# A fused attention and two-layer MLP kernel: every fourth addition into y goes from VectorE to a ScalarE copy and an accumulating DMA of GpSimd

## Chip, cores and metric

One core of a Trainium2 chip runs the whole kernel. The metric is the device time of one execution in microseconds (us). Engines are named as in the profile: PE (TensorE; PEld is its weight load), DVE (VectorE), ACT (ScalarE), POOL (GpSimd) and SP (SyncE, which here only issues DMAs).

## Reference

Attention over 4 sequences of 32 global and 512 local tokens, 8 heads of 64 (a local token sees the global tokens and the locals within 32 of it), and then two MLP layers with a squared ReLU:

```python
x = attn_out.transpose(0, 2, 1, 3).reshape(B * S, H * D)      # 2176 x 512
def _moe_ref(x, w_in, w_out):                                  # w_in 512 x 2048, w_out 2048 x 512
    h = x @ w_in
    r = np.maximum(h, 0.0)
    g = r * r
    return (g @ w_out).astype(np.float32)
x = _moe_ref(x=x, **moe_kwargs)
return _moe2_ref(x=x, **moe2_kwargs)                           # the same with other weights
```

## The kernel before

**Data.** Activations lie transposed: 512 features are four tiles of 128 partitions (index `d` or `k`), and the 2176 tokens are five blocks of 256, 512, 512, 448 and 448 columns (`NB`, blocks 0 to 4). Each fp32 operand is held as a high and a low part (`xh`/`xl`, `whi`/`wlo`, `gh`/`gl`), and each product is three matmuls (`three`, L565 to L567): high by high, high by low, low by high.

**Stages.** The first part is attention. The MLP then takes the 16 chunks of 128 hidden units of a layer two at a time. The first four chunks of layer 0 are done block by block; after them come 14 stages of two chunks each: 6 of layer 0 and 8 of layer 1. In a stage block 0 is computed directly (`first`), and the block pairs A = (1, 2) and B = (3, 4) by a scheme that trades products for sums of inputs and weights (`products`, `tsums`, `sums`). `activate` squares the ReLU and splits it (L585 to L591, L235). `second` multiplies the result by the chunk's `w_out` for each of the four `d`, into one PSUM bank for each: `Y0`, `PT0`, `PT1` and, for `d` = 3, `O0`.

**y.** `finish(d)` inside `second` moves a finished bank into the SBUF tile `y[b][:, d, :]`. For the first chunks of a layer it is a copy (L220). In the other stages, 6 of layer 0 and 7 of layer 1, it is an addition on DVE (L618): 13 stages x 5 blocks x 4 = 260 additions. After the last stage of layer 0 `y` is split into the inputs of layer 1 (L623, L625) and summed for the pairs (`tsums`, L725); after the last stage of layer 1 it is stored (L302).

**Staging tiles.** `staging()` hands out the `NR` tiles `r` of 128 x 512 in turn, to `activate` and to `products`.

**Order.** `Plan.add` records each operation with its engine, an assumed cost and a priority; `Plan.order` plays these costs forward, takes on each engine the ready operation of the best priority, and so fixes the order in which the instructions are written. Every engine then works through its own list strictly in that order. A changed cost or dependency therefore moves instructions on all engines from that point on.

```python
    def staging():
        i = cnt["r"] % NR
        cnt["r"] += 1
        return rt[i], ("r", i)
```

Of the kernel before, what the change touches and what calls it, by code (L numbers as in the profile page):

```python
# [13 lines left out]
AF = mybir.ActivationFunctionType  # L14
ALU = mybir.AluOpType
# [42 lines left out]
 'NS': 3,  # L58
 'NPT': 6,
 'NV': 2,  # L60
 'NR': 8,
 'NWR': 1,
 'NWT': 4,
 'Y': ['Y0'],
# [26 lines left out]
class Plan:  # L91
# [8 lines left out]
    def add(self, eng, cost, prio, fn, reads=(), writes=(), tail=0.0, lock=False, mode="M"):  # L100
        op = Op()
        op.eng, op.cost, op.prio, op.fn, op.tail, op.lock = eng, cost, prio, fn, tail, lock
        op.mode = mode
        op.seq = len(self.ops)
        deps = {}

        def dep(o, raw):
            if o is not None and o is not op:
                deps[o] = deps.get(o, False) or raw

        for r in reads:
            dep(self.writer.get(r), True)
        for w in writes:
            dep(self.writer.get(w), True)
            for o in self.readers.get(w, ()):
                dep(o, False)
        for r in reads:
            self.readers.setdefault(r, []).append(op)
        for w in writes:
            self.writer[w] = op  # L120
            self.readers[w] = []
        op.deps, op.users, op.left, op.ready = deps, [], len(deps), 0.0
        for o in deps:
            o.users.append(op)
        self.ops.append(op)
        return op

    def order(self):
        free, pend, avail = {}, {}, {}
        for op in self.ops:  # L130
            free.setdefault(op.eng, 0.55 if op.eng == "SP" else 0.0)
            pend.setdefault(op.eng, [])
            avail.setdefault(op.eng, [])
            if op.left == 0:
                heapq.heappush(pend[op.eng], (0.0, op.seq, op))
        done, dma, dmas, cols, port, tile_mode = [], 0.55, [], {}, {}, "M"
        while len(done) < len(self.ops):
            best = None
            for e in free:
                t = free[e] if avail[e] else (max(free[e], pend[e][0][0]) if pend[e] else None)  # L140
                if t is not None and (best is None or t < best[0]):
                    best = (t, e)
            t, e = best
            while pend[e] and pend[e][0][0] <= t:
                _, _, op = heapq.heappop(pend[e])
                heapq.heappush(avail[e], (op.prio, op.seq, op))
            op = heapq.heappop(avail[e])[2]
            if op.lock or e == "Pool":
                t = max(t, port.get("Pool" if e == "DVE" else "DVE", 0.0))
                port[e] = t + op.cost  # L150
            op.start, op.end = t, t + op.cost
            if e == "PE":
                n = int(t / TICK)
                op.end += switch(tile_mode, op.mode)
                tile_mode = op.mode
                if cols.get(n - 1, 0.0) < 3060:
                    op.end += op.cost * 0.95
                share, done_at = op.cost * 2400 / (op.end - t), t
                while done_at < op.end:
                    n = int(done_at / TICK + 1e-9)  # L160
                    upto = min(op.end, (n + 1) * TICK)
                    cols[n] = cols.get(n, 0.0) + share * (upto - done_at)
                    done_at = upto + 1e-9
            free[e] = op.end
            if e == "SP":
                if len(dmas) >= 8 and dmas[-8] > op.start:
                    op.start = dmas[-8]
                    free[e] = op.start + op.cost
                dma = max(dma, op.start + 1.1) + op.tail
                op.end = dma + 0.9  # L170
                dmas.append(op.end)
            done.append(op)
            for u in op.users:
                raw = u.deps[op]
                lat = LAT[e][u.eng] if u.eng != e or raw else 0.0
                u.ready = max(u.ready, op.end + lat)
                u.left -= 1
                if u.left == 0:
                    heapq.heappush(pend[u.eng], (u.ready, u.seq, u))
        self.total = max(o.end for o in done)  # L180
        return done


def switch(a, b):

    if a in "SVW":
        return 0.0 if a == b else 0.095 if b in "SVW" else 0.205 if b in "MG" else 0.145
    return 0.092 if b in "SVW" else 0.012 if a != b else 0.0


def dve(n, fast=False):
    return 0.065 + (0.53 if fast else 1.045) * n / 1000


def act(n):
    return 0.055 + 0.835 * n / 1000


def pe_r(n, m=128):
    return max(n + 32, 2 * m + 6) / 2400  # L200
# [3 lines left out]
def kernel(ctx: ExitStack, tc: tile.TileContext, kl, ql, vl, gk, gv, win, wout, msk, idn, out):  # L204
    nc = tc.nc
    plan = Plan()
    EARLY = CFG["EARLY"]
    add = plan.add
    picks = {}

    def pick(key):
        i = picks.get(key, 0)
        picks[key] = i + 1
        return CFG[key][i % len(CFG[key])]
# [40 lines left out]
    NR, NWR, NWT = (CFG[k] for k in ("NR", "NWR", "NWT"))  # L255
# [40 lines left out]
    def take(kind, names):  # L296
        k = names[cnt[kind] % len(names)]
        cnt[kind] += 1
        return k
# [264 lines left out]
    def three(out_, hi, lo, xhi, xlo, start, stop, again=False):  # L564
        nc.tensor.matmul(out=out_, lhsT=hi, rhs=xhi, start=start, stop=False, skip_group_check=again)  # L565
        nc.tensor.matmul(out=out_, lhsT=hi, rhs=xlo, start=False, stop=False, skip_group_check=again)  # L566
        nc.tensor.matmul(out=out_, lhsT=lo, rhs=xhi, start=False, stop=stop, skip_group_check=again)  # L567
# [5 lines that stand above are left out]
# [25 lines left out]
    def second(P, b, fs, slots, late, dfirst, stages):  # L598

        nb = NB[b]  # L600
        c3 = 3 * pe_r(nb)
        yk = [take("Y", CFG["Y"] + CFG["PT"] + CFG["O"] if late else CFG["Y"]) for _ in range(KD)]

        def passes(d, n):
            f, slot = fs[n], slots[n]
            o = bank[yk[d]][:, 0:nb]
            add("PE", c3, P(), lambda: three(o, wv(whi, slot)[:, d, :], wv(wlo, slot)[:, d, :], gh[f][:, 0:nb], gl[f][:, 0:nb],
                                             n == 0, n == len(fs) - 1), (("w", slot), ("gh", f), ("gl", f)), (yk[d],))

        def finish(d):  # L610
            o, yd = bank[yk[d]][:, 0:nb], y[b][:, d, :]
            Y = ("y", b, d)
            layer, begin, end = stages
            if begin:
                first = {1: (("gk", 0), ("gp", 0)), 2: (("gk", 1), ("gp", 1)), 3: (("gv", 0),), 4: (("gv", 1),)}.get(b, ())
                copy("yc", P(), yd, o, nb, (yk[d],), (Y,) + (first if layer == 0 else ()), psum=True)
                return
            add("DVE", dve(nb), P(), lambda: nc.vector.tensor_tensor(out=yd, in0=yd, in1=o, op=ALU.add), (yk[d],), (Y,))  # L618
            if end and layer == 0:
                if b in SECOND and d < 2:  # L620
                    return
                hi, lo = xh[b][:, d, :], xl[b][:, d, :]
                add("Activation", act(nb) + 0.04, P(), lambda: nc.scalar.activation(out=hi, in_=yd, func=AF.Copy),  # L623
                    (Y,), (("x", b, d),))
                add("DVE", dve(nb), P(), lambda: nc.vector.tensor_tensor(  # L625
                    out=lo, in0=yd, in1=hi.bitcast(F32), op=ALU.subtract), (Y,), (("x", b, d),), lock=True)
            elif end:
                load(P(), out[128 * d:128 * d + 128, OFF[b]:OFF[b] + nb], yd, 512 * nb, (Y,), ())

        N = len(fs)  # L630
        if dfirst:
            w = min(2, len(CFG["Y"]))
            for d0 in range(0, KD, w):
                for d in range(d0, d0 + w):
                    for n in range(N - 1):
                        passes(d, n)
                for d in range(d0, d0 + w):
                    passes(d, N - 1)
                    finish(d)
        else:  # L640
            for n in range(N):
                for d in range(KD):
                    passes(d, n)
                    if n == N - 1:
                        finish(d)
# [142 lines left out]
    for b in range(5):  # L788
        P = prios(MP[b], CFG["step"][b])
# [6 lines left out]
    for layer in range(2):  # L796
        for p in range(STAGES):
# [9 lines left out]
            for n, j in enumerate(order):  # L807
                P = prios(100 * (stage + 1) + 10 * n)
# [119 lines left out]
```

## Time and profile before

| | |
|---|---|
| median of 3 runs | 884.58 us (883.54 to 886.32) |
| profiled execution | 884.31 us, span 882.5 us from first to last instruction |
| granted TensorE clock | 1.00 |
| PE busy | 860.1 us, 97% of the span |
| DVE busy | 697.0 us, 79% |
| ACT busy | 551.3 us, 62% |
| POOL busy | 70.8 us, 8% |
| DMA | 67.92 MB, mean 77 GB/s |

Busy time says how long an engine had something in work, not whether it was waited for. "Idle before <- X" is time in which an engine stood still until X ended. The chain is followed back from the last instruction. The time outside the span (884.31 - 882.5 = 1.81 us) is start and end of the program.

### The profile page before, as it was taken

Reading aid. Unit: us, or ns where it says so; the run is one execution under the profiler, and the core shown is the slowest. Engines: PE = TensorE matmul, PEld = TensorE weight load, DVE = VectorE, ACT = ScalarE, POOL = GpSimd, SP = SyncE. Lnnn points to the kernel's source line nnn. Section 1 sums busy time; section 2 is a strip of 40 time slices with the busy share of each in tenths; the row PEclk is TensorE's granted clock in tenths of the full one; section 3 lists DMA queues with packets and bytes.
Section 4 is the critical chain, followed back from the end, with each engine's and each line's share of the span. In section 5 each row is a group of like instructions: output and inputs, shape, how many; then the busy total and the mean of one; then the engine's idle time right before and its main releaser. Section 6 shows DMA issues by size and latency. Waiting matters only on the chain.

```text
span 882.5 us, 14400 instructions
## 1 busy us (share of the span) xinstructions
PE 860.1 (97%) x5248; PEld 743.1 (84%) x5248; DVE 697.0 (79%) x1619; ACT 551.3 (62%) x1234; POOL 70.8 (8%) x116
## 2 busy tenths in 40 slices
PE   5999899999999999999999999999999999999998
PEld 4878686788888888898889889898988988898987
DVE  4988888753899798886877999788887777877544
ACT  4898789885675556535645779755554645554543
POOL 3333334320000000000000000000000000000000
PEclk9999999999999999999999999999999999999999
DMA  7877354420001121211110102112112020201023
GB/s 276 289 231 234 111 145 134 139 59 22 1 1 48 48 72 50 70 49 48 46 51 25 48 1 66 54 53 69 48 48 72 25 72 25 72 25 49 1 84 120
DMA packets 28071, 67.92 MB, mean 77 GB/s; under 512 B 3168, under 2 KB 13024, under 8 KB 28000
## 3 DMA queue, kind: packets, MB, share of 16 engines
q1 hardware_dynamic: 28000, 67.01, 24.2%
q8 instruction: 41, 0.67, 0.3%
q14 instruction: 30, 0.25, 0.1%
HBM read 62.54 MB, written 4.46 MB: 76 GB/s over the span
## 4 chain that ended last, share of the span: by engine, by line
PE 84%; ACT 6%; DVE 5%; DMA 3%; issue 1%; SPq 0%; POOL 0%; ACTq 0%; DVEq 0%
PE h L565 7%; PE h L566 7%; PE h L567 7%; PE PT L566 6%; PE PT L565 6%; PE PT L567 6%; PE S L565 5%; PE S L566 5%; PE S L567 5%; PE Y L565 4%; PE Y L566 4%; PE Y L567 4%; PE O L566 3%; PE O L567 3%; PE O L565 3%; PE O L382 2%
## 5 line engine op out<-in xcount | busy, mean ns | idle before, releaser
L235 DVE TENSOR_TENSOR gl<-r,gh 128x448 fp32r<-128x448 f32 (+2 forms) x160 | 96.6, 610 | 59.2 <-ACT r L589 57.9
L566 PE MATMUL PT<-gl,whi 128*128 128x448 f32 (+2 forms) x288 | 103.5, 359 | 0.0
L565 PE MATMUL PT<-gh,whi 128*128 128x448 f32 (+2 forms) x288 | 103.4, 359 | 0.0
L567 PE MATMUL PT<-gh,wlo 128*128 128x448 f32 (+2 forms) x288 | 103.3, 359 | 0.0
L520 ACT ACTIVATE whi<-wt 128x512 fp32r<-128x512 f32 x92 | 56.9, 623 | 73.6 <-PE S L566 34.6
L586 ACT ACTIVATE gh<-r 128x448 fp32r<-128x448 f32 (+2 forms) x160 | 89.1, 562 | 2.4 <-PE Y L567 0.2
L585 ACT ACTIVATE r<-r 128x512 f32<-128x512 f32 (+1 forms) x84 | 50.5, 601 | 61.7 <-DVE r L695 61.3
L589 ACT ACTIVATE r<-r 128x448 f32<-128x448 f32 (+2 forms) x145 | 82.2, 568 | 3.8
L565 PE MATMUL h<-xh,whi 128*128 128x512 f32 (+2 forms) x232 | 83.6, 360 | 0.6 <-ACT r L585 0.6
L618 DVE TENSOR_TENSOR y<-y,PT 128x448 f32<-128x448 f32 (+2 forms) x130 | 75.5, 600 | 9.2 <-PE PT L567 8.9
L566 PE MATMUL h<-xl,whi 128*128 128x512 f32 (+2 forms) x232 | 80.3, 346 | 2.4 <-DVE xl L396 2.3
L567 PE MATMUL h<-xh,wlo 128*128 128x512 f32 (+2 forms) x232 | 79.9, 344 | 0.0
L565 PE MATMUL Y<-gh,whi 128*128 128x512 f32 (+2 forms) x208 | 76.8, 369 | 0.2 <-ACT y L220 0.2
L566 PE MATMUL Y<-gl,whi 128*128 128x512 f32 (+2 forms) x208 | 75.0, 361 | 0.5 <-DVE gl L235 0.5
L235 DVE TENSOR_TENSOR wlo<-wt,whi 128x512 fp32r<-128x512 f32 x92 | 63.2, 690 | 14.8 <-ACT whi L520 14.4
L567 PE MATMUL Y<-gh,wlo 128*128 128x512 f32 (+2 forms) x208 | 74.6, 359 | 0.0
L351 ACT ACTIVATE s<-s,mn 128x224 f32<-128x224 f32 x128 | 60.2, 473 | 8.9 <-DVE mn L346 8.8
L565 PE MATMUL S<-xh,whi 128*128 128x448 f32 (+2 forms) x184 | 65.5, 356 | 0.0
L566 PE MATMUL S<-xl,whi 128*128 128x448 f32 (+2 forms) x184 | 65.3, 355 | 0.0
L567 PE MATMUL S<-xh,wlo 128*128 128x448 f32 (+2 forms) x184 | 65.1, 354 | 0.0
L566 PEld LDWEIGHTS PT<-gl,whi 128*128 128x128 f32 x288 | 54.3, 188 | 6.5 <-DVE gl L235 0.2
L565 PEld LDWEIGHTS PT<-gh,whi 128*128 128x128 f32 x288 | 54.3, 188 | 6.4
(129 smaller groups left out, 2125.0 us busy)
## 6 DMA issues: line engine op xcount, KB each, us to landing
wraw<-win SPq DMA_DIRECT2D x32, 512.0 KB, 3.5
wraw<-wout SPq DMA_DIRECT2D x32, 512.0 KB, 3.5
v<-vl SPq DMA_DIRECT2D x32, 224.0 KB, 2.7
rk<-kl SPq DMA_DIRECT2D x32, 192.0 KB, 2.9
y<-gk SPq DMA_DIRECT2D x8, 672.0 KB, 5.5
y<-gv SPq DMA_DIRECT2D x8, 640.0 KB, 6.9
rq<-ql SPq DMA_DIRECT2D x32, 128.0 KB, 2.5
out<-y SPq DMA_DIRECT2D x8, 256.0 KB, 2.0
```

The costliest lines, as they stand in the source:

```text
L235: add("DVE", dve(n), prio, lambda: nc.vector.tensor_tensor(out=get(out_), in0=get(a), in1=get(b), op=ALU.subtract), reads, writes, lock=True)
L351: add("Activation", 0.48, P(), lambda t=t, sb=sb: nc.scalar.activation(out=st[sb][:, t, :], in_=st[sb][:, t, :], func=AF.Exp, bias=mn[sb][ ...
L382: nc.tensor.matmul(out=bank[ok][64 * e:64 * e + 64, 128 * t:128 * t + 128], lhsT=vt[vb][:, 128 * k + 64 * e:128 * k + 64 * e + 64], rhs=pt ...
L520: nc.scalar.activation(out=whi[slot], in_=tf, func=AF.Copy)
L565: nc.tensor.matmul(out=out_, lhsT=hi, rhs=xhi, start=start, stop=False, skip_group_check=again)
L566: nc.tensor.matmul(out=out_, lhsT=hi, rhs=xlo, start=False, stop=False, skip_group_check=again)
L567: nc.tensor.matmul(out=out_, lhsT=lo, rhs=xhi, start=False, stop=stop, skip_group_check=again)
L585: add("Activation", act(nb), P(), lambda: nc.scalar.activation(out=r, in_=src, func=AF.Relu), (S,), (R,))
L586: add("Activation", act(nb) + 0.04, P(), lambda: nc.scalar.activation(out=a, in_=r, func=AF.Square), (R,), (("gh", f),))
L589: add("Activation", act(nb) + 0.04, P(), lambda: nc.scalar.activation(out=r, in_=r, func=AF.Square), (), (R,))
L618: add("DVE", dve(nb), P(), lambda: nc.vector.tensor_tensor(out=yd, in0=yd, in1=o, op=ALU.add), (yk[d],), (Y,))
```

## The change

A new setting `ya` = 'DDDM' is stepped through by the additions of `finish`. Since each block has four of them, the fourth, `d` = 3, always gets M: ACT copies bank `O0` to a staging tile, and POOL issues a DMA that adds this tile to `y[b][:, 3, :]` in SBUF. That is 65 of the 260 additions: 13 of 256, 26 of 448 and 26 of 512 columns. The staging tiles go from 8 to 7, the build's parameter `dynamic_dma_scratch_size` from 256 to 2048. The planner books the DMA with 1.2 on POOL and 3.0 more until it has landed; these two numbers are assumptions written in the code.

```diff
- 'NR': 8,
+ 'ya': 'DDDM',
+ 'NR': 7,
...
+            if e == "Pool":
+                op.end += op.tail
...
-            add("DVE", dve(nb), P(), lambda: nc.vector.tensor_tensor(out=yd, in0=yd, in1=o, op=ALU.add), (yk[d],), (Y,))
+            if pick("ya") == "M":
+                r, R = staging()
+                r = r[:, 0:nb]
+                add("Activation", act(nb), P(), lambda: nc.scalar.activation(out=r, in_=o, func=AF.Copy), (yk[d],), (R,))
+                add("Pool", 1.2, P(), lambda: nc.gpsimd.dma_start(out=yd, in_=r, accum_op=ALU.add), (R,), (Y,), tail=3.0)
+            else:
+                add("DVE", dve(nb), P(), lambda: nc.vector.tensor_tensor(out=yd, in0=yd, in1=o, op=ALU.add), (yk[d],), (Y,))
...
-    nc = _bacc.Bacc("TRN2", target_bir_lowering=False, num_devices=1, dynamic_dma_scratch_size=256)
+    nc = _bacc.Bacc("TRN2", target_bir_lowering=False, num_devices=1, dynamic_dma_scratch_size=2048)
```

In the changed kernel lines stand 3 to 9 further down: L220 is L223 there, L585 is L588, L618 is L627, and the new copy and DMA are L624 and L625. PE runs the same matmuls; their order is the same through attention and the first chunks and differs in places after that. The rows below are the instructions as written, with the semaphores that each waits for in brackets (Activation_49 is ACT's counter, DMASW a DMA issued by POOL, DMAHW one issued by SP).

**The end of the program.** The last rows of DVE before; `O_156` is the bank of `d` = 3, `y_74` is block 0:

```order
L235 TENSOR_TENSOR gl_86<-r_90,gh_82 128x256 [waits Activation_49]
L618 TENSOR_TENSOR y_74<-y_74,Y_151 128x256 [waits PE_49]
L618 TENSOR_TENSOR y_74<-y_74,PT_154 128x256 [waits PE_49]
L618 TENSOR_TENSOR y_74<-y_74,PT_155 128x256 [waits PE_49]
L618 TENSOR_TENSOR y_74<-y_74,O_156 128x256 [waits PE_49]
```

The last rows of ACT now (`O_155` is the same bank):

```order
L624 ACTIVATE r_91<-O_155 128x512 [waits DVE_49,PE_49]
L588 ACTIVATE r_89<-S_151 128x256 [waits DMASW4_49,PE_49]
L589 ACTIVATE gh_81<-r_89 128x256 [waits Activation_49]
L588 ACTIVATE r_90<-S_152 128x256 [waits PE_49]
L589 ACTIVATE gh_82<-r_90 128x256 [waits Activation_49]
L592 ACTIVATE r_90<-r_90 128x256 [waits Activation_49]
L624 ACTIVATE r_92<-O_155 128x256 [waits PE_49]
```

The last rows of POOL now:

```order
L625 DMA y_77<-r_89 128x448 [waits DMASW2_49,Activation_49]
L625 DMA y_78<-r_87 128x448 [waits DMASW3_49,Activation_49]
L625 DMA y_75<-r_88 128x512 [waits DMASW0_49,Activation_49]
L625 DMA y_76<-r_91 128x512 [waits DMASW7_49,DMASW1_49,Activation_49]
L625 DMA y_74<-r_92 128x256 [waits Activation_49]
```

The last addition of the program has moved from DVE to a copy on ACT and a DMA on POOL.

**The stores behind it.** SP's last rows before:

```order
L302 DMA out<-y_76 128x512 [waits DMAHW1_49,DVE_49]
L302 DMA out<-y_74 128x256 [waits DMAHW2_49,DVE_49]
L302 DMA out<-y_74 128x256 [waits DMAHW3_49,DVE_49]
L302 DMA out<-y_74 128x256 [waits DMAHW4_49,DVE_49]
L302 DMA out<-y_74 128x256 [waits DMAHW5_49,DVE_49]
```

And now:

```order
L305 DMA out<-y_76 128x512 [waits DMAHW1_49,DMASW7_49]
L305 DMA out<-y_74 128x256 [waits DMAHW2_49,DVE_49]
L305 DMA out<-y_74 128x256 [waits DMAHW3_49,DVE_49]
L305 DMA out<-y_74 128x256 [waits DMAHW4_49,DVE_49]
L305 DMA out<-y_74 128x256 [waits DMAHW5_49,DMASW0_49]
```

The very last store now waits for a DMA of POOL to have landed, where it waited for DVE.

**A staging tile taken again.** ACT in the first of the 14 stages, now (`r_91` receives a bank of `d` = 3 and is written again five rows later):

```order
L624 ACTIVATE r_91<-O_155 128x512 [waits PE_49]
L523 ACTIVATE whi_101<-wt_96 128x512 [waits DVE_49]
L624 ACTIVATE r_89<-O_155 128x512 [waits PE_49]
L223 ACTIVATE r_87<-h_149 128x448 [waits PE_49,Activation_49]
L588 ACTIVATE r_92<-r_92 128x448 [waits DVE_49]
L223 ACTIVATE r_91<-h_148 128x512 [waits DMASW1_49,PE_49,Activation_49]
```

ACT at the same place before:

```order
L494 ACTIVATE wraw_95<-wraw_95 128x512 [waits DMAHW7_49,DVE_49]
L520 ACTIVATE whi_107<-wt_97 128x512 [waits DVE_49]
L585 ACTIVATE r_93<-r_93 128x448 [waits DVE_49]
L220 ACTIVATE r_94<-h_150 128x448 [waits PE_49]
L586 ACTIVATE gh_81<-r_93 128x448 [waits Activation_49]
L589 ACTIVATE r_93<-r_93 128x448 [waits Activation_49]
L220 ACTIVATE r_89<-h_149 128x512 [waits PE_49]
```

The copy of a PSUM bank of products into `r_91` (L223) now waits for the DMA that reads the tile's earlier content; before, such copies waited for PE and the compute engines alone. In all, 4 of the 65 tiles are written again on ACT within 10 rows, and 9 within 15.

## Rows read from the trace of the kernel before

**Rows 1.** The page: span, and busy time of each engine.
```profile
span 882.5 us, 14400 instructions
PE 860.1 (97%) x5248; PEld 743.1 (84%) x5248; DVE 697.0 (79%) x1619; ACT 551.3 (62%) x1234; POOL 70.8 (8%) x116
```

**Rows 2.** Busy time by stretch (start:end, length, engines, PEclk, DMA share, GB/s).
```profile
250.00:300.00 50.00, 48.61 (x240) 42.03 (x239) 47.18 (x88) 31.34 (x60) 0.00 (x0) 1.00 0.11 32
500.00:550.00 50.00, 50.00 (x254) 44.10 (x253) 49.85 (x89) 40.52 (x81) 0.00 (x0) 1.00 0.11 32
850.00:882.50 32.50, 28.70 (x149) 24.51 (x147) 14.41 (x25) 10.86 (x20) 0.00 (x0) 1.00 0.32 118
300.00:850.00 550.00, 549.80 (x2805) 486.31 (x2804) 445.97 (x812) 310.64 (x590) 0.00 (x0) 1.00 0.16 48
```

**Rows 3.** Waits of PE from 230 us on (total us, times, longest).
```profile
PE S L565 <- ACT r L220: 1.4, 2, 0.7
PE Y L566 <- DVE gl L235: 0.5, 2, 0.3
PE Y L565 <- ACT y L220: 0.2, 1, 0.2
```

**Rows 4.** Groups by form: DVE's additions from bank O (busy us, mean ns | idle before).
```profile
L618 DVE TENSOR_TENSOR y<-y,O 128x512 f32<-128x512 f32 x26 | 17.7, 680 | 4.0 <-PE O L567 4.0
L618 DVE TENSOR_TENSOR y<-y,O 128x448 f32<-128x448 f32 x26 | 15.9, 613 | 1.8 <-PE O L567 1.8
L618 DVE TENSOR_TENSOR y<-y,O 128x256 f32<-128x256 f32 x13 | 5.4, 414 | 0.6 <-PE O L567 0.6
```

**Rows 5.** Groups by form: ACT's copies out of bank O.
```profile
L220 ACT ACTIVATE y<-O 128x512 f32<-128x512 f32 x2 | 1.2, 604 | 0.8 <-PE O L567 0.8
L220 ACT ACTIVATE y<-O 128x448 f32<-128x448 f32 x3 | 1.6, 538 | 0.1
L220 ACT ACTIVATE y<-O 128x256 f32<-128x256 f32 x1 | 0.4, 384 | 0.3 <-PE O L567 0.3
```

**Rows 6.** Timeline of PE, bank O used twice near the end (start us, us).
```profile
867.59 0.39 PE L567 MATMUL O<-gh,wlo 128*128 128x512 f32 x1
867.82 0.39 PE L565 MATMUL Y<-gh,whi 128*128 128x512 f32 x1
...
871.90 0.39 PE L565 MATMUL O<-gh,whi 128*128 128x512 f32 x1
```

**Rows 7.** Timeline of the last 5 us: last matmul, last addition, last stores.
```profile
878.40 1.79 SPq L302 DMA_DIRECT2D out<-y  x4
...
878.71 0.28 PE L567 MATMUL O<-gh,wlo 128*128 128x256 f32 x1
879.02 0.42 DVE L618 TENSOR_TENSOR y<-y,O 128x256 f32<-128x256 f32 x1
```

**Rows 8.** One line's instructions, SP's stores: duration min/median/max ns; landing us.
```profile
L302 SPq DMA_DIRECT2D out<-y x20: 332/333/403, 847.4 to 879.8; - x20
DMA to landing us min/median/max: 1.7/2.0/2.2
```

**Rows 9.** DMA issues (KB each, median us from issue to landing).
```profile
y<-gk SPq DMA_DIRECT2D x8, 672.0 KB, 5.5
...
out<-y SPq DMA_DIRECT2D x8, 256.0 KB, 2.0
...
out<-y SPq DMA_DIRECT2D x4, 128.0 KB, 1.8
```

**Rows 10.** Groups by form on POOL, the longest of it.
```profile
L238 POOL TENSOR_TENSOR lk<-rk,hk 128x384 fp32r<-128x384 f32 x21 | 23.4, 1113 | 14.8 <-DVE hk L223 7.7 <-issue 2.8 <-ACT hk L220 2.0
```

**Rows 11.** Groups by form on DVE from 200 us on: first step of the weights.
```profile
L484 DVE TENSOR_SCALAR wt<-wraw 128x512 uint32<-128x512 uint32 x52 | 21.9, 422 | 10.5 <-DMA wraw<-wout 6.0 <-DMA wraw<-win 4.0
```

## The prediction

> **What bounds the kernel now.** I read the page's busy times first [rows 1]: PE has work for 860.1 of 882.5 us, DVE for 697.0, ACT for 551.3, and POOL for 70.8. A share over the whole span says little, so the second view is busy time by stretch [rows 2]. From 300 to 850 us, which holds nearly all additions into y, PE is busy 549.80 of 550 us at a granted clock of 1.00, with DVE at 445.97 and ACT at 310.64. The reader is to see that DVE may be full for 50 us (49.85 from 500 to 550) while PE still misses nothing. The third view, the waits of PE [rows 3], gives what a faster DVE or ACT could return after 230 us: 1.4 + 0.5 + 0.2 = 2.1 us, of which 1.4 stand behind ACT. That a busy PE could hide waits is a fair objection; matmuls on 512 columns start 0.23 us apart (867.59 and 867.82 [rows 6]), and 512 columns at 2.4 GHz are 0.213 us, so little is hidden. The kernel is bound by PE up to its last matmul; behind that stands a tail that nothing covers [rows 7]. It is the place to price.
>
> **The base.** The profiled execution took 884.31 us: span 882.5 and 1.81 around it. The median of the runs is 884.58, so 0.27 above; I add to 884.31. What can be told from no change is 0.3%, here 2.65 us.
>
> **DVE loses 65 additions.** By form [rows 4]: 26 x 0.680 + 26 x 0.613 + 13 x 0.414 = 17.7 + 15.9 + 5.4 = 39.0 us less on DVE. Worth on the path: 0. PE runs beside them; the most they could give back is the 0.5 us in which PE waited for DVE [rows 3].
>
> **ACT gains 65 copies.** The same copy exists in the kernel, from bank O with the same three widths [rows 5]: 26 x 0.604 + 26 x 0.538 + 13 x 0.384 = 15.7 + 14.0 + 5.0 = 34.7 us more on ACT. Cost on the path: 0, hidden by PE, since ACT has 239 us free from 300 to 850 [rows 2]. If that cover goes, the copy is late and PE waits for bank O. Near the end the last matmul on O starts at 867.59 and ends at 867.98, and the next one on O starts at 871.90 [rows 6]: 3.9 us, for a copy of 0.6, so some five queued ACT operations fit ahead of it.
>
> **POOL gains 65 DMAs**, and nothing stands in their way there: its 70.8 us belong to attention, and from 250 us on it does nothing [rows 1, 2]. They carry 14.5 MB (26 x 256 KB + 26 x 224 KB + 13 x 128 KB), and the DMA must read y as well, while the engines' queues are 16% busy between 300 and 850 us [rows 2]. Cost 0; weights could come a little later, and nobody is near that bound.
>
> **Staging tiles.** Seven instead of eight, 65 more takers, and a tile is free only when the DMA has read it. The list of ACT in the changed program shows 4 of the 65 tiles written again within 10 rows, the closest five rows later. At some 0.6 us a row that is 3 us, in an engine that works strictly in order; behind a late tile its squares and weight copies queue up, and PE waits for those. With the DMA length I take below this costs at most a few tenths: 0 in the sum. The splits of y between the layers also wait for such DMAs, but the inputs are needed by PE later than the DVE work that lies between; also 0.
>
> **The end.** Here every step lies on the path. Before [rows 7]: the last matmul starts at 878.71 and ends at 878.99, DVE adds from 879.02 to 879.44, and SP's four stores end their issue at 878.40 + 1.79 = 880.19. With 0.33 for an issue [rows 8] the last one starts at 879.86, 0.42 after the addition; it ends the span 2.3 us later, at 882.5. Now ACT copies in 0.384 instead of DVE's 0.414 [rows 4, 5]: nothing gained or lost. POOL then has to notice, issue, and the DMA has to land before SP may start the last store. For noticing I take what SP needed behind DVE, 0.42. For issue to landing no row shows a DMA of POOL or one that adds. The lower end is SP's own store of the same 128 KB: 1.8 [rows 9]. The upper end is its load of 672 KB, five times the bytes: 5.5 [rows 9]. I take 3.1, nearer the lower end because the bytes are those of the short row: 1.8, plus 1.1 for POOL to prepare it (its slowest group of instructions takes 1.113 each [rows 10]; what an issue costs it no row shows), plus 0.2 because y is read too (256 KB against 128 KB on SP: 2.0 against 1.8 [rows 9]). The tail grows by 0.42 + 3.1 = **3.5 us**, with ends at 2.2 and 5.9. The planner's own assumption of 1.2 + 3.0 would make it 4.6.
>
> The Trainium skill (DMA: Bandwidth & Descriptors, section on the anatomy of a DMA on the GpSimd path) has a fit of 2.0 us plus bytes / 436e3 for such a DMA: an estimate of 2.3 us for 131,072 bytes. By it the sum below would be 887.0, inside what counts as no change. No run here shows a DMA of POOL yet.
>
> **Sum.** 884.31 + 0 (DVE) + 0 (ACT) + 0 (POOL, staging) + 3.5 (end) = **887.8 us**, 3.2 above the median (0.36%). With the ends of the DMA's length: 886.5 to 890.2.
>
> **Rivals.**
>
> *The end is short, and a relieved DVE helps (not slower).* One mechanism: the DMA takes about what SP's stores take, so the tail grows by 2.2 to 2.7 us. In addition the stretch from 250 to 300 us may run better, where DVE is 94% busy and PE idle for 1.39 us [rows 2]. For it: the same bytes leave SBUF in 1.8 us on SP, and that stretch does depend on DVE. Against: the 1.4 us there stand behind ACT [rows 3], which gets no relief, one staging tile fewer makes such waits likelier, and POOL's preparation is left out. It gives 885.1 (1.4 won, 2.2 lost) to 887.0. It decides at a growth of the tail of 2.9 us: below that, the time is within 0.3% of 884.58. Chance 0.36, in which I count the short end of my own range. The fit of the Trainium skill above falls in this case.
>
> *Faster.* To get below 881.9 the program must win 2.4 us and the tail's growth back, at least 4.6 together. PE's waits after 230 us are 2.1 [rows 3], and earlier the program is the same. That leaves only waits hidden in busy time. Chance 0.04.
>
> *The DMAs land late, and the staging tiles bind (slower by more).* If a DMA takes 6 us or more in the middle of the program, the tiles taken again within 10 rows come late by some 3, 2, 1 and 1 us, ACT stands still, and PE waits for about half of it: 3 to 4 us, on top of a longer tail of up to 6. It gives 890 to 894. What could do it: weight loads of 512 KB in front of it on the same engines, or DVE. For it: POOL's part is unknown here. Against: the planner places each reuse where its assumed 4.2 us have passed, so the wait begins only beyond that. It decides at about 5 us from issue to landing. Chance 0.12.
>
> The Trainium skill (SBUF — State Buffer, section on the two separate sides) says that GpSimd cannot write the descriptors of a DMA while DVE runs an operation in a mode that takes both ports, and would have them late in this way. The trace so far has no such DMA; DVE's operations of the likely kind take 0.42 us each [rows 11], so one of them alone delays little.
>
> *The forecast itself*, a tail of 2.9 to 5.9 and little else: 0.48, all of it slower by over 0.3%.
>
> **How the numbers follow.** Slower by over 0.3%: 0.48 + 0.12 = 0.60. Within 0.3%: 0.36. Faster: 0.04. The predicted time is that of the likeliest case, 887.8. The range reaches down into the short tail, to 885.4, and up through the longer DMA into half of the late one, to 892.0; about one in ten is left out on either side. The likeliest case alone lies at 887.2 to 890.2.
>
> **What would show it.** In the changed profile: DVE down by about 39 us and ACT up by about 35; 65 DMAs on POOL with a landing time of about 3 us for 128 KB; PE still over 549 of 550 us from 300 to 850; and in the last 8 us the order matmul, ACT copy, DMA of POOL, last store, with 7.0 us from the end of the last matmul to the end of the span, against 3.5 before (878.99 to 882.5). The forecast is wrong if PE shows waits for ACT that end with DMASW events between 250 and 850 us, if the tail grows by under 2.9 us, or if PE's part before the last matmul gets shorter by more than 2 us.

## The result, and the profile after

| | before | changed |
|---|---|---|
| median, 18 runs each on the same chips | 885.98 us (882.56 to 889.05) | 892.24 us (887.84 to 896.80) |
| ratio, 95% interval | | 1.0070 (1.0053 to 1.0088) |
| profiled execution | 884.31 us, span 882.5 | 887.84 us, span 886.0 |

The change costs 6.3 us by the medians. The forecast was 887.8 with a range of 885.4 to 892.0: the sign was right, the size half of what came, and the time lies just outside the range. Of the 4.4 us between 892.24 and 887.8, 1.7 lie in the base: the sum started at the profiled execution, 884.31, and the kernel before has a median of 885.98 here. The first profiled execution took 887.84, the forecast to the hair, and that is an accident: it is the fastest of its 18 runs. Its attention part was 2.4 us faster than in the profile of before, with the same instructions in the same order: the two traces first differ at about 223 us, on DVE. Against the prediction stands the median.

The page of the changed kernel answers to [rows 1]:

```profile
span 886.0 us, 14604 instructions
## 1 busy us (share of the span) xinstructions
PE 860.5 (97%) x5248; PEld 742.8 (84%) x5248; DVE 667.3 (75%) x1554; ACT 584.8 (66%) x1299; POOL 128.6 (15%) x181
```

The 65 additions left DVE (1554 instructions for 1619), the 65 copies came to ACT, PE has the same work. Busy time by stretch in the changed kernel, as [rows 2] (DVE, ACT and POOL are the third to fifth busy times, then PEclk, DMA share, GB/s):

```profile
300.00:850.00 550.00, 547.97 (x2795) 484.65 (x2794) 420.68 (x757) 341.01 (x649) 48.24 (x56) 1.00 0.30 70
850.00:886.00 36.00, 29.59 (x154) 25.32 (x152) 12.78 (x22) 13.00 (x24) 4.07 (x5) 0.98 0.51 148
```

Between 300 and 850 us PE now misses 2.03 us, where it missed 0.20 [rows 2]; the DMA engines are busy 30% where it was 16%. The waits of PE from 230 us on, as [rows 3]:

```profile
PE h L568 <- ACT r L223: 1.4, 2, 0.9
PE h L568 <- ACT r L588: 0.9, 1, 0.9
PE S L568 <- ACT r L223: 0.7, 1, 0.7
PE Y L569 <- DVE gl L238: 0.6, 2, 0.3
PE PT L569 <- DVE gl L238: 0.2, 1, 0.2
PE S L568 <- DVE r L704: 0.2, 1, 0.2
```

That is 4.0 us in place of 2.1. The end of the program in the timeline (start us, us), as [rows 7]:

```profile
878.75 4.90 SPq L305 DMA_DIRECT2D out<-y  x5
...
879.60 0.28 PE L570 MATMUL O<-gh,wlo 128*128 128x256 f32 x1
879.92 0.38 ACT L624 ACTIVATE r<-O 128x256 f32<-128x256 f32 x1 [2.13 <-PE O L570]
880.66 0.86 POOL L625 DMA_DIRECT2D y<-r  x1 [4.35 <-ACT r L624]
```

From the start of the last matmul to the end of the span it is 886.0 - 879.60 = 6.40 us, where it was 882.5 - 878.71 = 3.79 [rows 7]: 2.6 us more. The new DMAs themselves, in the page's list of DMA issues (KB, median us to landing) and as the instructions of their line (duration min/median/max in ns, then landing in us):

```profile
y<-r POOLq DMA_DIRECT2D x26, 256.0 KB, 3.3
...
y<-r POOLq DMA_DIRECT2D x26, 224.0 KB, 3.2
...
y<-r POOLq DMA_DIRECT2D x13, 128.0 KB, 2.7
```
```profile
L625 POOL DMA_DIRECT2D y<-r x65: 852/862/1087, 271.4 to 880.7; - x65
...
DMA to landing us min/median/max: 2.6/3.3/6.0
```

To compare executions I cut each in three: **attention**, to the start of its last group of matmuls (L382 before, L385 in the changed kernel); **body**, from there to the start of the last matmul of the program; **tail**, from there to the end of the span. Each cut is a start time on PE in the timeline. For attention these are, before and in the changed kernel:

```profile
217.59 1.09 PE L382 MATMUL O<-pt,v 112*64 112x128 f32 x16
```
```profile
215.19 1.09 PE L385 MATMUL O<-pt,v 112*64 112x128 f32 x16
```

| kernel | tiles | adds by DMA | attention | body | tail |
|---|---|---|---|---|---|
| before | 8 | 0 | 217.59 | 661.12 | 3.79 |
| changed | 7 | 65 | 215.19 | 664.41 | 6.40 |

So 2.6 us were lost in the tail and 3.3 in the body; attention hid 2.4 of them.

### The profile page after: what moved, and what is told of

It reads as the page before. It is cut to its first block, busy times and chain, and to the rows that moved or that the text cites. A ratio compares the mean times of both kernels' runs of the same rounds, so it can differ in the third digit from the quotient of the medians.

```text
span 886.0 us, 14604 instructions
## 1 busy us (share of the span) xinstructions
PE 860.5 (97%) x5248; PEld 742.8 (84%) x5248; DVE 667.3 (75%) x1554; ACT 584.8 (66%) x1299; POOL 128.6 (15%) x181
## 4 chain that ended last, share of the span: by engine, by line
PE 79%; DVE 8%; ACT 6%; DMA 4%; issue 2%; SPq 0%; POOL 0%; POOLq 0%; ACTq 0%; DVEq 0%
PE h L568 7%; PE h L569 7%; PE h L570 7%; PE PT L568 6%; PE PT L570 6%; PE PT L569 6%; PE S L568 4%; PE S L569 4%; PE S L570 4%; PE Y L568 4%; PE Y L569 4%; PE Y L570 4%; PE O L568 3%; PE O L570 3%; PE O L569 3%; PE O L385 2%
## 5 line engine op out<-in xcount | busy, mean ns | idle before, releaser
L625 POOL DMA_DIRECT2D y<-r x65 | 56.8, 874 | 616.2 <-ACT r L624 569.8
L624 ACT ACTIVATE r<-O 128x512 f32<-128x512 f32 (+2 forms) x65 | 34.6, 533 | 118.9 <-PE O L570 118.9
L627 DVE TENSOR_TENSOR y<-y,PT 128x448 f32<-128x448 f32 (+2 forms) x130 | 76.2, 605 | 19.2 <-PE PT L570 18.6
L588 ACT ACTIVATE r<-r 128x512 f32<-128x512 f32 (+1 forms) x84 | 50.4, 600 | 28.7 <-DVE r L704 28.6
```

The costliest lines, as they stand in the source:

```text
L588: add("Activation", act(nb), P(), lambda: nc.scalar.activation(out=r, in_=src, func=AF.Relu), (S,), (R,))
L624: add("Activation", act(nb), P(), lambda: nc.scalar.activation(out=r, in_=o, func=AF.Copy), (yk[d],), (R,))
L625: add("Pool", 1.2, P(), lambda: nc.gpsimd.dma_start(out=yd, in_=r, accum_op=ALU.add), (R,), (Y,), tail=3.0)
```

## The experiments

Two theories at the start. The medians were 4.4 us above the profiled execution, and the runs' mean granted clocks went from 0.999 (887.84 us) to 0.990 (896.80 us). Theory 1: the change makes PE wait, the granted clock falls after it, and that is most of the loss. Theory 2: all of it lies behind the last matmul. The seven staging tiles were a third suspect. All timed ratios are against the kernel before on the same chip, with a 95% interval.

**a_again: the changed kernel once more.** No edit.

> The changed kernel again, for a second profiled execution. The first took 887.84 us at a mean granted clock of 0.999, while the 18 runs have a median of 892.24 at clocks of 0.990 to 0.999. Theory 1 (clock): an ordinary execution shows 890 to 893 us at a clock near 0.995, with stretches of a lower PEclk between 250 and 850 us that begin just after PE has waited for ACT or DVE. Theory 2 (the end alone): the added time lies behind the last matmul; any lower clock stands in the last 10 us, and the last matmul ends at about 880 us as in the first profile.

891.34 us: attention 219.27, body 663.81, tail 6.42. Neither theory holds for this execution. Up to the last matmul PEclk was below 1.00 only in attention, at 90 to 100 us, where the instructions are those of the kernel before. Yet body and tail repeat the loss: 2.7 and 2.6 us. One profile does not settle theory 1 for the median, though. The 70 runs of the kernel before whose mean granted clock is on record stand at 0.998 in the middle, the 18 of the changed kernel at 0.996, and its longer tail, in which PE stands still, explains at most 0.001 of that (0.98 over the last 36 us, above). In the kernel before, the 26 runs at 1.000 have a median of 884.15 us and the 25 at 0.998 one of 886.06, so a part of the 6.3 us goes with a lower clock; where it fell in the runs without a profile is not known.

**e1_end_dve: the last stage back on DVE.**

```diff
-            if pick("ya") == "M":
+            if pick("ya") == "M" and not (end and layer == 1):
```

> The changed kernel with DVE additions in the last stage only (60 DMAs instead of 65); PE's list of instructions is the same. The profile of the change shows 6.1 us from the end of the last matmul to the end of the span, against 3.5 before, so 2.6 us should go. Theory 1 (most of the rest is lost clock in the body): 889 to 890 us, still some 3 to 4 us above the kernel before, at clocks near 0.995. Theory 2 (the end alone): equal to the kernel before within 1 us.

888.89 us, 1.0033 (1.0018 to 1.0048); body 663.34, tail 3.87. The tail is worth 2.5 us in the trace and about 3.3 by the ratios. What is left, about 2.9 us, is near theory 1 in size (3 to 4); the lower clock in its profile (50 to 60 and 95 to 100 us) stands in attention again.

**e3_seven: nothing but the missing tile.**

```diff
- 'NR': 8,
+ 'NR': 7,
```

> The kernel before with seven staging tiles instead of eight, all additions on DVE; PE's list is that of e2_end_only. If the lost staging tile is what makes PE wait (and then run at a lower clock): 889 to 890 us. If the copies on ACT and the DMAs do it: within 1 us of the kernel before.

887.60 us, 1.0023 (1.0004 to 1.0042); body 662.16, tail 3.86. The tile alone costs 1.0 us of body in the trace (1.6 against b_again below) and 2.0 by the ratio, about a third of the whole change, without one DMA of POOL; the interval, 0.4 to 3.7 us, is wide. The missing tile also changes the planned order: PE's list of instructions is another from 231 us of the kernel before on, in the last of the first chunks. PE's waits after 230 us come to 2.7 us for 2.1 [rows 3], and the longest is new:

```profile
PE h L565 <- ACT r L585: 1.1, 1, 1.1
```

All seven 7-tile profiles show this wait for ACT's L588 (L585 here), with 0.9 to 1.1 us, and none of the five 8-tile profiles. The cause in the changed kernel's timeline, ACT and PE by time:

```profile
253.97 0.58 ACT L741 ACTIVATE tBh<-r 128x448 fp32r<-128x448 f32 x1 [1.61 <-DVE r L734]
...
255.30 0.39 PE L570 MATMUL h<-xh,wlo 128*128 128x512 f32 x1
...
256.20 0.38 ACT L588 ACTIVATE r<-h 128x256 f32<-128x256 f32 x1 [1.64 <-DVE r L734]
...
256.63 0.47 PE L568 MATMUL h<-xh,whi 128*128 128x448 f32 x1 [0.94 <-ACT r L588]
```

And ACT at the same work in the kernel before:

```profile
253.22 0.42 ACT L586 ACTIVATE gh<-r 128x256 fp32r<-128x256 f32 x1
253.67 0.42 ACT L589 ACTIVATE r<-r 128x256 f32<-128x256 f32 x1
253.99 0.37 ACT L585 ACTIVATE r<-h 128x256 f32<-128x256 f32 x1
...
258.95 0.60 ACT L220 ACTIVATE r<-S 128x512 f32<-128x512 f32 x1 [1.77 <-DVE r L725]
```

The ReLU that empties bank h needs a staging tile. With seven it gets one only after DVE's sums for the block pairs (L734, L725 before) are through with it: ACT stands for 1.64 us, bank h stays full, PE stands behind it. With eight the same ReLU runs with no wait. That the wait is for the tile is read from its operands: the ReLU reads h, which comes from PE, and the one thing of DVE that it touches is `r`. The last line shows that eight are short too: a copy out of bank S, which reads nothing of DVE either, waits 1.77 us for a tile.

**e2_end_only: seven tiles, DMAs in the last stage alone.** Only 5 DMAs are left.

```diff
+            if pick("ya") == "M" and end and layer == 1:
```

> The kernel before with seven staging tiles and the accumulating DMAs in the last stage alone (5 instead of 65). Theory 1: the end costs 2.6 us and nothing else does, so 2 to 3 us above e3_seven, and clocks like those of the kernel before. Theory 2: 6 us above e3_seven, all that the change costs.

890.88 us, 1.0055 (1.0033 to 1.0077): 3.3 us above e3_seven, nearer to theory 1 (2 to 3) than to theory 2 (6), but at clocks of 0.995 to 0.997, below the middle of the kernel before; tail 6.35. Its body of 663.90 is 1.7 above e3_seven, with the same list of PE. The stretches say why (PE, PEld, DVE, ACT, POOL busy, PEclk, DMA share, GB/s):

```profile
255.00:260.00 5.00, 3.90 (x18) 2.92 (x17) 5.00 (x10) 1.59 (x4) 0.00 (x0) 1.00 0.00 0
260.00:265.00 5.00, 4.32 (x13) 3.30 (x13) 4.92 (x10) 3.16 (x8) 0.00 (x0) 0.69 0.00 0
265.00:270.00 5.00, 4.99 (x22) 3.91 (x22) 3.89 (x8) 4.42 (x9) 0.00 (x0) 0.97 0.01 3
```
```profile
259.78 0.47 PE L568 MATMUL h<-xh,whi 128*128 128x448 f32 x1 [1.10 <-ACT r L588]
...
261.95 0.79 PE L568 MATMUL S<-tAh,whi 128*128 128x512 f32 x1 [0.68 <-ACT r L223]
262.54 0.63 PE L569 MATMUL S<-tAl,whi 128*128 128x512 f32 x1
...
263.39 0.63 PE L568 MATMUL S<-tAh,whi 128*128 128x512 f32 x1
263.82 0.63 PE L569 MATMUL S<-tAl,whi 128*128 128x512 f32 x1
```

PE waited 1.10 and 0.68 us close together, and then matmuls on 512 columns start 0.43 us apart instead of 0.23: the lower level, 1.2 GHz. This is theory 1 in small: with a tile missing, a stretch of low clock can follow the waits. It shows in two of seven 7-tile profiles (here and in e6_copy_dve) and in none of the five 8-tile profiles at this place; so few profiles suggest that the tile brings it, and do not show it.

**b_again: the kernel before once more.** No edit.

> The kernel before again, for a second profiled execution. In five profiles so far attention ended between 2.4 us earlier and 4.2 us later than in the first profile of this kernel, with PEclk below 1.00 at 50 to 60 or 90 to 100 us in three of them. If the change causes that lower clock: attention as in the first profile, clock 1.00 throughout, about 884 us. If it is scatter of every kernel: attention ends some us later or earlier, and the time from there to the end is 672 us again, within 0.5.

882.70 us: attention 216.51, body 660.59, tail 3.80. Body and tail repeat within 0.6, as the expectation had it for scatter (its 672 us count from an earlier group of matmuls, which ends at 210.5 us). The clock stayed at 1.00 here, so in profiles attention scatters without the change by only 1.1 us; but the runs of this kernel on record without a profile have clocks from 0.992 to 1.000, so it has stretches of lower clock too. Lower clock in attention shows in five of the profiles (a_again, e1_end_dve, e2_end_only, e3_seven, e7_eight_end_dve), with seven tiles and with eight, and in e3_seven with no DMA of POOL at all; the new instructions are not needed for it.

**e4_eight: the change with eight tiles.**

```diff
- 'NR': 7,
+ 'NR': 8,
...
-    nc = _bacc.Bacc("TRN2", target_bir_lowering=False, num_devices=1, dynamic_dma_scratch_size=2048)
+    nc = _bacc.Bacc("TRN2", target_bir_lowering=False, num_devices=1, dynamic_dma_scratch_size=512)
```

> The changed kernel with eight staging tiles (room for the eighth comes from the reserved 2048, now 512). Theory A (the missing tile makes PE wait at about 258 us, 1.1 us, and at times for a stretch of lower clock behind it): that wait goes, 1 to 2 us less than the change, 890 to 891. Rival B (the tile does not matter, the copies and DMAs do): the wait stays or comes back elsewhere, 892.

887.07 us, 1.0027 (1.0011 to 1.0043); body 661.03, tail 6.41. Both theories had it slower (890 to 891, 892). The interval lies below that of the change (1.0053 to 1.0088), though it overlaps that of the change's second timing (a_timed below, from 1.0039). The body is back at that of before, with all 65 DMAs in it, and the middle clock at 0.998. Rival B is out: with the DMAs in, one tile makes up 0.35 to 0.43% of the 0.62 to 0.70%. The reserved 2048 went down to 512 in the same step; no run changes that alone, but e6_copy_dve below keeps 2048, without DMAs, and costs nothing that can be measured. The waits of PE from 230 us on in this kernel:

```profile
PE h L568 <- ACT r L223: 1.4, 2, 0.9
PE S L568 <- ACT r L223: 1.0, 2, 0.5
PE Y L569 <- DVE gl L238: 0.3, 1, 0.3
PE Y L568 <- ACT y L223: 0.2, 1, 0.2
```

The wait for L588 is gone. Others are new (0.9 at 507 us, 0.45 at 415), and the two that before had at 258 and 263 us are shorter (0.5 each for 0.7 [rows 3]). The shorter ones give back 0.4 of 1.35; the waits come to 2.9 us for 2.1 before, while the bodies are equal, and what makes up the rest is not shown. Nor do the waits explain all that the tile gave back: they fell by 1.1 us from the change, the body by 2.8 to 3.4.

**e6_copy_dve: copies on ACT, additions on DVE, seven tiles.**

```diff
-                add("Pool", 1.2, P(), lambda: nc.gpsimd.dma_start(out=yd, in_=r, accum_op=ALU.add), (R,), (Y,), tail=3.0)
+                add("DVE", dve(nb), P(), lambda: nc.vector.tensor_tensor(out=yd, in0=yd, in1=r, op=ALU.add), (R,), (Y,), lock=True)
```

> As e1_end_dve, but DVE adds the staging tile to y instead of the DMA: the copies on ACT stay, the 60 DMAs and their landing times go, and DVE gets its 60 additions back. From the end of attention to the last stage e1_end_dve took 1.2 us more than e3_seven. If the load on ACT makes PE wait: 888 to 889, as e1_end_dve. If the landing times or the DMA traffic do: 887 to 888, as e3_seven. If DVE is the bound somewhere, slower than both.

886.25 us, 1.0010 (0.9994 to 1.0025), below all three expectations, though its profile has the low clock at 260 us (body 663.23, of it some 1.5 by that, an estimate from 5 us at 0.66). ACT carries the 60 copies, and PE misses 0.48 us of 550:

```profile
300.00:850.00 550.00, 549.52 (x2805) 486.91 (x2804) 446.13 (x810) 341.61 (x650) 0.00 (x0) 1.00 0.15 47
```

So the load on ACT is not what costs. It also bounds the tile: this kernel has seven, with the wait of 1.1 us, and its interval includes no loss at all. Without DMAs the missing tile costs 0.9 us here and 2.0 in e3_seven; the larger part appears only with the DMAs. The intervals of e1_end_dve, e3_seven and this one overlap, so their order is not shown by times; in the profiles the DMAs go with 1.2 us of body (e1_end_dve against e3_seven), the copies with none. Where such a wait comes from in the changed kernel (POOL's DMA, SP's load, then DVE, ACT and PE, by time):

```profile
407.86 0.86 POOL L625 DMA_DIRECT2D y<-r  x1 [13.05 <-ACT r L624]
...
408.02 0.33 SPq L305 DMA_DIRECT2D wraw<-wout  x1
...
412.87 0.43 DVE L487 TENSOR_SCALAR wt<-wraw 128x512 uint32<-128x512 uint32 x1 [1.57 <-DMA wraw<-wout]
413.33 0.69 DVE L489 SCALAR_TENSOR_TENSOR wt<-wraw,wt 128x512 uint32<-128x512 uint32 x1
413.94 0.68 DVE L704 TENSOR_TENSOR r<-r,S 128x512 f32<-128x512 f32 x1
...
414.66 0.63 ACT L588 ACTIVATE r<-r 128x512 f32<-128x512 f32 x1 [1.63 <-DVE r L704]
415.19 0.58 ACT L223 ACTIVATE r<-h 128x512 f32<-128x512 f32 x1
...
415.82 0.50 PE L568 MATMUL h<-tAh,whi 128*128 128x512 f32 x1 [0.50 <-ACT r L223]
```

A load of weights follows an accumulating DMA by 0.2 us and lands 4.8 us after its issue, where the median of these loads is 3.7; the DMA itself lands after 6.0, the longest of all 65, where the median for its 224 KB is 3.2. DVE waits 1.57 us for it; the product's sum (L704) behind it is late, ACT behind that, and PE waits 0.50 us behind ACT. DVE's waits for weights from 230 us on, in the changed kernel and in the one before:

```profile
DVE wt L487 <- DMA wraw<-win: 9.5, 9, 1.6
DVE wt L487 <- DMA wraw<-wout: 5.2, 5, 1.7
```
```profile
DVE wt L484 <- DMA wraw<-wout: 6.0, 6, 1.9
DVE wt L484 <- DMA wraw<-win: 4.0, 5, 2.2
```

They fit, but e6_copy_dve has 14.3 us of them with no DMA of POOL, so waits of DVE alone prove nothing; that the two DMAs slow each other is read from this place and from another at 612 us (5.3 us for the DMA, 5.6 for the load issued 0.9 us behind it), and was not tested apart.

**e5_nine: nine tiles in the kernel before.** For room, a tile of weights in preparation less.

```diff
- 'NR': 8,
+ 'NR': 9,
...
- 'NWT': 4,
+ 'NWT': 3,
```

> The kernel before with nine staging tiles and three instead of four tiles for weights in preparation. Theory A: if staging tiles bind near 258 us, a ninth takes some of the 1.4 us that PE still waits there for ACT: up to 1.5 us faster than the kernel before. Rival: those waits are DVE work itself, no change; or the missing weight tile costs more, 1 to 3 us slower.

899.16 us, 1.0157 (1.0132 to 1.0182). Much slower, by some 14 us; of the rivals the one on the weight tile fits (1 to 3 us slower), and it was far too low. The longest waits of PE name that tile's users:

```profile
PE Y L565 <- ACT whi L520: 1.9, 1, 1.9
PE S L567 <- DVE wlo L235: 1.0, 1, 1.0
```

What a ninth tile is worth stays open, since two things were changed at once.

**a_timed, e7_eight_end_dve, e8_eight_mid: the sum.** The first is the changed kernel. The second is e4_eight with the edit of e1_end_dve; the third has this line:

```diff
+            if pick("ya") == "M" and not end:
```

> The changed kernel, timed beside the next two on one chip. By the profiles it costs 2.6 us at the end and 2 to 3 us between the end of attention and the last stage: 5 to 7 us above the kernel before, 890 to 892.

> The changed kernel with eight staging tiles and DVE additions in the last stage, so 60 copies and DMAs and nothing else. Theory (the missing tile and the end are the whole cost): within 1 us of the kernel before, though DVE has 36 us less to do, since PE bounds. Rival (the copies and DMAs cost 1 to 2 us by themselves, as e1_end_dve against e3_seven suggests): 886.5 to 887.5, and PE waits at 414 and 507 us that are not made up elsewhere.

> As e7_eight_end_dve, with DVE additions in the last stage of layer 0 too (55 DMAs are left). In e4_eight PE waited 0.9 us at 507 us, where the splits of y wait for a DMA. If that wait hangs on the DMAs, it goes, and the kernel is up to 1 us below e7_eight_end_dve and perhaps below the kernel before. If it comes from the order alone, it stays.

| kernel | tiles | DMAs | us | ratio (interval) | attention | body | tail |
|---|---|---|---|---|---|---|---|
| a_timed | 7 | 65 | 890.51 | 1.0062 (1.0039 to 1.0085) | 218.14 | 663.86 | 6.40 |
| e4_eight | 8 | 65 | 887.07 | 1.0027 (1.0011 to 1.0043) | 216.66 | 661.03 | 6.41 |
| e7_eight_end_dve | 8 | 60 | 886.25 | 1.0009 (0.9988 to 1.0030) | 220.47 | 661.58 | 3.85 |
| e8_eight_mid | 8 | 55 | 885.60 | 1.0000 (0.9981 to 1.0018) | 217.26 | 661.01 | 3.93 |

With eight tiles and the end on DVE, 60 of 65 DMAs cost nothing that can be measured, and gain nothing. The interval of e7_eight_end_dve, -1.1 to +2.7 us, still leaves room for its rival's 1 to 2 us. In e8_eight_mid the wait at 507 us is gone, as expected if it hangs on the DMAs, but one of 0.7 us at 550 took its place; it is not faster than the kernel before. No version here is measurably faster than that one.

## Why the prediction was wrong

**Staging tiles: the step that failed.** The prediction looked at tiles held by DMAs, "the closest five rows later", and put "0 in the sum". A tile binds elsewhere: at the start of the 14 stages, before the first DMA is issued (271 us), seven tiles are too few for the sums of the block pairs, and PE waits 0.9 to 1.1 us and then 0.7, where with eight it waited twice 0.7 or less. The body loses 1.0 to 1.6 us by the missing tile alone (e3_seven against the two profiles of before) and 2.7 to 3.3 with the DMAs (a_again, a_timed and the first profile against the first of before); two profiles have a stretch at 1.2 GHz behind the wait, some 1.5 us. By the times it is 2.0 us alone in e3_seven, with none in e6_copy_dve's interval, and 3.1 to 3.8 within the change. Why a missing tile costs more beside the DMAs than alone stays open. The waits of PE in [rows 3] had named the place: 1.4 of its 2.1 us were waits for ACT there already. The prediction noted under its rivals that one tile fewer "makes such waits likelier", and gave that no price. Base 885.98, tail 2.6 and body 2.7 to 3.3 come to 891.3 to 891.9, of the 892.24 measured.

**The end** was right as a mechanism and too large. 3.5 was forecast, 2.6 came (e4_eight and every other kernel with the end on POOL), below the 2.9 that the prediction named as a sign of being wrong. ACT's copy took 0.38 as said. POOL started 0.36 after it (0.42 forecast). The DMA landed after 2.7 us, for 3.1. The last store's issue started at 878.75 + 4.90 - 0.33 = 883.32, just as the DMA landed (880.66 + 2.7), so the 0.42 that SP needed behind DVE [rows 7, 8] was not paid a second time: the forecast had counted it in the old tail and left it in the new one. The Trainium skill's fit (DMA: Bandwidth & Descriptors, on the anatomy of a DMA on the GpSimd path) gave an estimate of 2.3 for this DMA; measured are 2.7, and 3.3 for 256 KB where it gives 2.6. Here the fit is low by 0.4 and 0.7; whether the addition into y makes the difference was not tested.

**DVE, ACT, POOL at 0** held, within what can be measured, once the tile was given back (e7_eight_end_dve). That PE was the bound, so 39 us off DVE are worth nothing, was the right reading of [rows 2]. ACT rose by 33.5 us for a forecast of 34.7. DVE's busy time fell by 29.7 and not by 39.0: instructions of DVE overlap (at 413.33 and 413.94 above they start 0.61 us apart, and the first lasts 0.69), and the groups' times [rows 4] count overlaps twice. Whether that is the whole difference was not worked out.

**"PE still over 549 of 550 us"** was the test named in advance, and it failed: 547.97. The weights that "could come a little later, and nobody is near that bound" came 0.1 to 0.2 us later by the median (3.6 and 3.7 for 3.5 on the pages), and at 408 us by 1.1, in front of a DVE that works in order.

**Rivals.** The short end had the tail right (2.2 to 2.7), but not the change: no relief by DVE shows in its times. The late DMAs had the right size (890 to 894) by luck: single DMAs did land late, up to 6.0 us, but in the changed kernel's list of waits nobody waits for an accumulating DMA but POOL itself, once, for 4.7 us. The Trainium skill's rule on descriptors that GpSimd cannot write while DVE uses both ports (SBUF — State Buffer, on the two separate sides) would have the DMAs late. Their issues on POOL took 852 to 1087 ns, so at most 0.2 us of it is in there; whether any of the late landings comes from it no run isolates.

## What to carry to other kernels

Price what a change takes for itself, here one buffer, as carefully as what it does: a wait that the trace already shows on a buffer's user tells where to look for the cost of one fewer. Work moved off an engine that hardly anybody waits for gained nothing here, while the one instance of it at the very end, where nothing covers it, was paid in full. And cut executions at the same instructions before comparing them: here 2.4 us of scatter in a part with the same instructions made a wrong forecast look exact.

## What was not expected of the hardware

- Two waits of PE, 1.1 and 0.68 us with 1.5 us of matmuls between them, were followed by some 3 us in which matmuls on 512 columns started 0.43 us apart (1.2 GHz) in two profiles, and by no such stretch in five others with the same two waits (0.9 to 1.1 and 0.7).
- Attention, with the same instructions, began its last group of matmuls between 215.2 and 221.8 us in the profiles above (e5_nine apart, whose order differs), and the five latest (218.3 us and later) are the five with slices of lower clock there.
- POOL was busy 0.86 us for each accumulating DMA, whatever its size (862 ns by the median), and the median landing time grew from 2.7 us for 128 KB to 3.3 for 256 KB.
